# Two layers of linear attention and a Mish block on one core: key folds in two packets, two fetches and one product moved

## The chip, the cores and the metric

The kernel runs on one core of a Trainium2 chip. The metric is the device time of one execution in microseconds (us), as the median of several runs. The core has five engines that take their instructions in order: TensorE (PE, with its weight loads shown apart as PEld), VectorE (DVE), ScalarE (ACT), GpSimd (POOL) and SyncE (SP), which issues the DMA transfers here. [...]

## The reference, cut to what matters

The input x has 2048 rows of 640 numbers. The program runs two layers, each made of an attention part A and a dense part B, both with a residual:

```python
x = x + _A_ref(_layernorm(x), A_wqkv, A_w_phi, A_wo)
x = x + _B_ref(_layernorm(x), B_w1, B_b1, B_w2)
# and both once more
```

A makes q, k and v with 32 heads of 20, and turns q and k by one 20 x 20 matrix per head (`w_phi`). The features of a head are the softmax of the result beside the softmax of its negative. Then `kv = phi_k^T v`, `z = sum of phi_k`, and the output of a row is `phi_q kv / (phi_q z + 1e-6)`, multiplied by `wo`. B is `mish(x w1 + b1) w2` with 1536 hidden columns.

## The kernel before, in words

**Blocks and stages.** Rows are worked in NB = 8 blocks of 256 (BT = 2 tiles of 128). Each layer has three stages: `attend_first` (norm, keys, values, queries, and the sum `kva` over all rows), `attend_second` (the average of each row, `wo`, the residual, the statistics of the next norm) and `dense` (part B). Every number stands as a high and a low float32r part, so each product takes three matmuls (`project_half`, L385: high x high, high x low, low x high), five chunks of 128 deep.

**Folding.** Instead of turning q and k by `w_phi`, the kernel multiplies the weights by it once: `fold_part` (L257) is a float32 matmul of one group of six heads for one chunk k, and `fold_end` (L272) takes the result out of PSUM, as a copy on ACT (L275, the high part) and a subtraction on DVE (L276, the low part). A fold has five chunks k and two column halves c; one pair (k, c) takes three `fold_part`s. The query folds are in a block `written()`, in which the engines keep the order of the code. The key folds are `fold_phi` (L278), called in block 0 ahead of the first keys (L586).

**PSUM.** There are two `mm` tiles of two banks each and four `one` tiles of one bank. A product that finds no free tile waits until ACT and DVE have emptied one. `fold_phi` gives an even k an `mm` tile and an odd k two `one` tiles.

**Stage one, per block** (L565): six kinds in a fixed list, for block 0 of layer 0 `q0, v0, v1, k0, q1, k1`. For each kind the products are issued, and `advance()` (L447) takes every earlier generator one step further: `features` (L402) copies the products (L409), then takes maximum and minimum (L416) and the differences (L417, L419), then the exponential, then sums, reciprocal and quotient (L425, L426, L427); `queries` then transposes on DVE (L478) and writes the result to `e_d` in four transfers (L481). `fetch_normed` (L438) fetches the next block's rows and makes their statistics (L295, L297, L304, L305, L307); `normed` (L345) normalizes them, and `nxt.step()` (L316) transposes them on PE (L325), with a copy on ACT (L330) and a subtraction on DVE (L331).

**What sets the order.** Outside the written block a planner orders each engine's list, from the order of the code and a model of durations. `tc.issue_after(ins)` puts the instructions traced in it that run on the engine of `ins` behind `ins`; those on other engines stay free. In stage two PE and SP keep the order of the code (L728), and the planner orders the rest.

**Start of layer 0** (L499): SP fetches the rows, `w_phi` and the weights; the statistics of block 0 are made; PE folds q's first half for k = 0 to 3 (L524); then come the first `fold_end` (L527), the normalization of block 0 (L529 on ACT, L530 on DVE), two more `fold_end`s, the transposes and the first half of q0's product (L544). The second half folds follow with the splits of v's weights between them (`make_v`, L546), and then q0's second half (L556).

**Stage two** (L728): `rest()` finishes the last queries of stage one; `load(b)` (L639) reads block b of `e_d` into two `big` tiles and an `ol` tile; `average` (L676, products at L690) makes the rows' averages; `Transposed(...).all()` turns them; `Rows.half` (L717) multiplies by half of `wo`, adds the residual rows `xs[b]` (L720) and takes statistics (L721). The rows are fetched with `fetch` (L430) into one of two `xt` buffers, `xs[0]` at L733 and `xs[b + 1]` at L767. `tail()` (L671) takes `rest()` a step further. Blocks 0 and 1 are averaged before the loop; inside it the order on PE is: first half for tile 0, second half for tile 0, transposes of block b + 1, both halves for tile 1, then averages for b + 2 and b + 3 in every second block.

Of the kernel before, what the change touches and what calls it, by code (L numbers as in the profile page):

```python
# [25 lines left out]
BT = 2  # L26
# [18 lines left out]
def kernel(  # L45
# [71 lines left out]
    last_act, in_written, last_low, last_load, last_recip = [None], [False], [None], [None], [None]  # L117
# [139 lines left out]
    def fold_part(ps, k, t, bd, raw):  # L257

        r, rows = raw[t]
        heads = rows // DH  # L260
        n = DL * (6 * (t % 3) if t < 5 else 10)
        nc.tensor.matmul(ps[:, n:n + heads * DL].rearrange("p (j d) -> p j d", d=DL), r[:rows, k * P:(k + 1) * P],
                         bd[:rows, t, :rows].rearrange("p (j d) -> p j d", d=DH)[:, :, :DL], start=True, stop=True)

# [7 lines left out]
    def fold_end(ws, ps, k, c):  # L272
        n0, n1 = (0, 18 * DL) if c == 0 else (18 * DL, QK)
        hi, lo = ws[k][0][:, n0:n1], ws[k][1][:, n0:n1]
        nc.scalar.activation(hi, ps[:, :n1 - n0], AF.Copy)  # L275
        nc.vector.tensor_tensor(lo, ps[:, :n1 - n0], hi.bitcast(F32), op=ALU.subtract)  # L276

    def fold_phi(ws, bd, raw):  # L278

        pss = {}  # L280
        for k, c in ((0, 0), (1, 0), (2, 0), (3, 0), (0, 1), (1, 1), (2, 1), (3, 1), (4, 0), (4, 1)):
            if c == 0:
                mm = None if k % 2 else mm_tile()
                pss[k] = [one_tile(), one_tile()] if k % 2 else [mm[:, 0], mm[:, 1]]
            ps = pss[k][c]
            for t in range(3 * c, 3 * c + 3):
                fold_part(ps, k, t, bd, raw)
            fold_end(ws, ps, k, c)
# [96 lines left out]
    def project_half(ps, xts, t, ws, col, c, ks=range(KD), w=HC):  # L385
        sl = slice(t * P, (t + 1) * P)
        cs = slice(col + c * w, col + (c + 1) * w)
        for k in ks:
            h, l, wh, wl = xts.hs[k], xts.ls[k], ws[k][0][:, cs], ws[k][1][:, cs]
            for n, (a, r) in enumerate(((h, wh), (h, wl), (l, wh))):  # L390
                nc.tensor.matmul(ps[:, :w], a[:, sl], r, start=(k == 0 and n == 0),  # L391
                                 stop=(k == KD - 1 and n == 2))
# [42 lines left out]
    def attend_first(layer, x_src, first):  # L435


        def fetch_normed(b):  # L438
            if layer:
                return load_turned(n2_d[b], [row_tile] * 3, nc.gpsimd)  # L440
            xt = fetch(x_src, b) if b > 1 else early
            norm_scale(b, [norm_stats(t, xt) for t in range(BT)])
            return xt
# [55 lines left out]
        if first is None:  # L499
            with written():  # L500
# [23 lines left out]
                for t in range(3):  # L524
                    for k in range(KD - 1):
                        fold_part(pcs[k], k, t, bd, raw_q)
                fold_end(q_ws, pcs[0], 0, 0)  # L527
# [3 lines left out]
                                        op0=ALU.mult, op1=ALU.add)  # L531
                fold_end(q_ws, pcs[1], 1, 0)
# [32 lines left out]
        for b in range(NB):  # L565
# [15 lines left out]
            for n, (kind, t) in enumerate(order):  # L581
                t = int(t)
                i = b * BT + t
                if b == 0 and n == (1 if layer else 3):
                    if layer == 0:
                        fold_phi(kv_ws, bd, raw)  # L586
                    kva = one_tile()
                    nc.vector.memset(kva[:, :360], 0.0)
                if b == NB - 1 and n == 3:
                    loaded = {0: load(0)}  # L590
                if b + 1 < NB:
# [8 lines left out]
                if b == NB - 1 and n == 3:  # L600
# [36 lines left out]
        return kva, o_ws, loaded, rest()  # L637
# [28 lines left out]
    def attend_second(x_src, x_dst, acc, fetches, makes, fetch_next, begin_next):  # L666
        kva, o_ws, loaded, rest = acc
# [60 lines left out]
        with tc.manual_schedule(engines={mybir.EngineType.PE, mybir.EngineType.SP}):  # L728
# [4 lines left out]
            xs = {0: fetch(x_src, 0)}  # L733
# [22 lines left out]
            for b in range(NB):  # L756
# [9 lines left out]
                if b + 1 < NB:  # L766
# [8 lines left out]
                if b == NB - 2:  # L775
                    ahead = begin_next()
                if b + 1 < NB:
# [3 lines left out]
                r1.half(0, one_tile())  # L781
# [256 lines left out]
```

## Time and profile before

| | |
|---|---|
| runs | 1360.75 us median of 3 (1360.6 to 1360.98) |
| profiled execution | 1362.07 us |
| its span, first to last instruction | 1360.3 us |
| granted TensorE clock | 1.000 over the span |
| ACT busy, POOL busy | 575.6 us, 462.9 us |
| DMA | 174.11 MB, mean 128 GB/s |

Every kind of line is a view of one profiled execution. In a **timeline** a line is: start, us, engine, line of the kernel, operation, output <- input with their shapes, xcount, and in square brackets how long the engine had been idle just before, and what ended that. In the list of **waits** it is: who waited, for whom, total us, times, longest. A line of **windows** gives a stretch, the busy us of PE, PEld, DVE, ACT and POOL (with instruction counts), the granted clock, the busy share of the 16 DMA engines and GB/s. SPq is SP's issue of a transfer, not the transfer. Tile names: `mm` and `one` in PSUM, `r2h/r2l` the query weights, `r1h/r1l` the key and value weights, `xth/xtl` the transposed rows, `big` and `r` the features, `xn` normalized rows or averages.

### The profile page before, as it was taken

What the parts mean: (1) busy time and instruction counts of PE and PEld (TensorE: products, weight loads), DVE (VectorE), ACT (ScalarE), POOL (GpSimd) and SP (SyncE); (2) the same over time, 40 slices, a digit from 0 to 9 for tenths busy, and PEclk for the clock granted to TensorE, in tenths of its full rate; (3) what the DMA queues carried; (4) which work ended last, traced back from release to release, by engine and by line L of the source; (5) the groups of instructions that cost most, each with busy time, mean ns of one, the idle gap of its engine ahead of it and who ended that gap; (6) DMA issues with size and microseconds to landing.
All of it is one profiled execution on the core that took longest, in us unless ns stands there. A gap on an engine that the chain in (4) does not pass through costs nothing.

```text
span 1360.3 us, 30985 instructions
## 1 busy us (share of the span) xinstructions
PE 1347.8 (99%) x12896; PEld 1336.8 (98%) x12896; DVE 1061.9 (78%) x1799; ACT 575.6 (42%) x967; POOL 462.9 (34%) x417
## 2 busy tenths in 40 slices
PE   9999999999999999999999999999999999999999
PEld 8899999999999999999999999999999999999998
DVE  5888988886687887778769788878668776677775
ACT  4444344312454545445443334332235444454443
POOL 2355654434222222222225555644251211111112
PEclk9999999999999999999999999999999999999999
DMA  9543433797714442244563534559974321333200
GB/s 336 153 107 79 98 92 85 206 287 271 222 42 98 117 110 76 60 107 99 145 210 78 121 79 89 97 116 290 280 248 136 78 61 44 91 98 97 65 33 20
DMA packets 352629, 174.11 MB, mean 128 GB/s; under 512 B 287449, under 2 KB 324041, under 8 KB 352489
## 3 DMA queue, kind: packets, MB, share of 16 engines
q1 hardware_dynamic: 352489, 172.14, 46.8%
q8 instruction: 101, 1.65, 0.5%
q14 instruction: 39, 0.32, 0.1%
HBM read 106.23 MB, written 65.86 MB: 127 GB/s over the span
## 4 chain that ended last, share of the span: by engine, by line
PE 91%; DVE 4%; DMA 1%; POOL 1%; issue 0%; ACT 0%; SPq 0%; DVEq 0%; POOLq 0%
PE one L813 25%; PE mm L391 25%; PE mm L864 24%; PE one L391 11%; PE mm L690 2%; PE one L325 2%; PE one L464 1%; DVE r L425 1%; PE one L864 1%; DVE m L416 1%; DMA ol<-e_d 1%; PE one L690 1%; DVE r L419 1%; POOL big L427 0%; DMA big<-e_d 0%
## 5 line engine op out<-in xcount | busy, mean ns | idle before, releaser
L864 PE MATMUL mm<-r2h,ol 128*128 128x320 f32 x1240 | 296.1, 309 | 0.0
L839 POOL TENSOR_TENSOR ol<-big,ol 128x512 fp32r<-128x512 f32 (+1 forms) x98 | 130.9, 1336 | 477.9 <-ACT ol L838 419.8
L813 PE MATMUL one<-xtl,r1h 128*128 128x256 f32 x960 | 268.2, 279 | 0.0
L813 PE MATMUL one<-xth,r1l 128*128 128x256 f32 x960 | 268.0, 279 | 0.0
L813 PE MATMUL one<-xth,r1h 128*128 128x256 f32 x960 | 265.9, 279 | 0.0
L864 PEld LDWEIGHTS mm<-r2h,ol 128*128 128x128 f32 x1240 | 212.4, 188 | 0.0
L864 PE MATMUL mm<-r2l,ol 128*128 128x320 f32 x620 | 191.2, 309 | 0.0
L391 PE MATMUL mm<-r1h,xth 128*128 128x304 f32 (+1 forms) x600 | 185.2, 309 | 1.5 <-DVE r1l L276 1.5
L391 PE MATMUL mm<-r1l,xth 128*128 128x304 f32 (+1 forms) x600 | 183.8, 306 | 0.0
L391 PE MATMUL mm<-r1h,xtl 128*128 128x304 f32 (+1 forms) x600 | 183.5, 306 | 0.2 <-POOL xtl L331 0.2
L813 PEld LDWEIGHTS one<-xtl,r1h 128*128 128x128 f32 x960 | 180.4, 188 | 0.0
L813 PEld LDWEIGHTS one<-xth,r1l 128*128 128x128 f32 x960 | 180.4, 188 | 0.0
L813 PEld LDWEIGHTS one<-xth,r1h 128*128 128x128 f32 x960 | 179.6, 188 | 0.0
L828 DVE TENSOR_SCALAR big<-big 128x512 f32<-128x512 f32 (+1 forms) x98 | 56.9, 580 | 110.3 <-ACT big L826 110.1
L427 POOL TENSOR_TENSOR r<-r,r 128x1280 f32<-128x1280 f32 x32 | 77.2, 2412 | 127.0 <-DVE r L426 112.0
L830 ACT ACTIVATE big<-big,two 128x512 f32<-128x512 f32 (+1 forms) x98 | 70.1, 716 | 116.2 <-DVE big L829 116.2
L838 ACT ACTIVATE ol<-big 128x512 fp32r<-128x512 f32 (+1 forms) x98 | 60.9, 622 | 137.7 <-DVE big L837 137.6
L826 ACT ACTIVATE big<-one,b1s 128x256 f32<-128x256 f32 x192 | 80.8, 467 | 89.2 <-PE one L813 88.7
L864 PEld LDWEIGHTS mm<-r2l,ol 128*128 128x128 f32 x620 | 116.5, 188 | 0.0
L391 PEld LDWEIGHTS mm<-r1h,xth 128*128 128x128 f32 x600 | 112.8, 188 | 2.6 <-DVE r1l L276 1.7
L391 PEld LDWEIGHTS mm<-r1h,xtl 128*128 128x128 f32 x600 | 112.8, 188 | 0.4 <-POOL xtl L331 0.4
L391 PEld LDWEIGHTS mm<-r1l,xth 128*128 128x128 f32 x600 | 112.8, 188 | 0.1
(155 smaller groups left out, 3144.3 us busy)
## 6 DMA issues: line engine op xcount, KB each, us to landing
e_d<-r SPq DMA_DIRECT2D x128, 160.0 KB, 4.1
big<-e_d SPq DMA_DIRECT2D x32, 640.0 KB, 8.1
x_d<-xt SPq DMA_DIRECT2D x23, 640.0 KB, 4.2
xt<-x_d SPq DMA_DIRECT2D x22, 640.0 KB, 5.4
n_d<-xn SPq DMA_DIRECT2D x168, 80.0 KB, 2.4
xt<-in_x SPq DMA_DIRECT2D x16, 640.0 KB, 4.3
xn<-x_d SPq DMA_DIRECT2D x28, 320.0 KB, 4.3
v<-n_d SPq DMA_DIRECT2D x30, 256.0 KB, 3.1
```

Of the source, the lines that this page charges most:

```text
L325: nc.tensor.transpose(ps[:, c, t * P:(t + 1) * P], self.rows[t][:, (c0 + c) * P:(c0 + c + 1) * P], ident)
L391: nc.tensor.matmul(ps[:, :w], a[:, sl], r, start=(k == 0 and n == 0), stop=(k == KD - 1 and n == 2))
L416: nc.vector.tensor_reduce(m[:, s], eh[:, 1], axis=AX.X, op=op)
L427: nc.gpsimd.tensor_tensor(eg, eg, r.unsqueeze(2).to_broadcast([P, 2 * H, DH]), op=ALU.mult)
L690: nc.tensor.matmul(po[c][64 * q:64 * q + 64, GW * j:GW * j + w], phs[g][:n, s0:s0 + 64], kvb[:n, g, :w], start=True, stop=True)
L813: nc.tensor.matmul(ph[:, j, :], l, r, start=(n == 0), stop=(n == 3 * KD - 1))
L826: exps[0] = nc.scalar.activation(part(ta, 0)[:, j - js.start], ph[:, j, :], AF.Exp, bias=b1s[:, 2 * pr + j:2 * pr + j + 1]).ins
L828: nc.vector.tensor_scalar_min(e, e, E_CAP)
L830: nc.scalar.activation(r, n, AF.Ln, bias=two)
L838: nc.scalar.activation(ah[:, js], n, AF.Copy)
L839: nc.gpsimd.tensor_tensor(al[:, js], n, ah[:, js].bitcast(F32), op=ALU.subtract)
L864: ins = nc.tensor.matmul(pys[t][c][:, :HC], (ah, ah, al)[n][:, j, t * P:(t + 1) * P], w, start=(f == 0 and n == 0), stop=(f == KF - 1 and ...
```

## The change

It has four parts.

1. In the written start, the first `fold_end` of the query folds is put behind the two normalizations of block 0.
2. The key folds are called in two packets: (0,0), (1,0), (2,0), (3,0) between v0 and v1, and (4,0), (0,1), (1,1), (2,1), (3,1), (4,1) between v1 and k0. Two folds at a time share an `mm` tile (the last two take `one` tiles), and their `fold_end`s follow both. Every packet, and every kind's products in block 0, is put behind the last product before it on PE. From the fifth kind on, `advance()` in block 0 is put behind the last `fold_end` on DVE, and so are the statistics of block 3.
3. `xs[0]` and `xs[1]` are fetched in stage one's last block, right behind `load(0)`, in both layers; the two later fetches of these blocks go.
4. In stage two's block 0, in both layers, the first half for tile 1 is put ahead of the transposes of block 1.

The cut diff:

```diff
@@ fold_part
-        nc.tensor.matmul(ps[:, n:n + heads * DL]...
+        ins = nc.tensor.matmul(ps[:, n:n + heads * DL]...
+        last_product[0] = ins.ins
@@ fold_end
-        nc.vector.tensor_tensor(lo, ps[:, :n1 - n0], hi.bitcast(F32), op=ALU.subtract)
+        last_fold[0] = nc.vector.tensor_tensor(lo, ps[:, :n1 - n0], hi.bitcast(F32), op=ALU.subtract).ins
-    def fold_phi(ws, bd, raw):
-        pss = {}
-        for k, c in ((0, 0), (1, 0), (2, 0), (3, 0), (0, 1), (1, 1), (2, 1), (3, 1), (4, 0), (4, 1)):
...
+    def fold_phi(ws, bd, raw, parts):
+        for n in range(0, len(parts), 2):
+            mm = mm_tile() if n < 4 else None
+            pair = list(zip(parts[n:n + 2], [one_tile(), one_tile()] if mm is None else [mm[:, 0], mm[:, 1]]))
+            with tc.issue_after(last_product[0]):
+                for (k, c), ps in pair:
+                    for t in range(3 * c, 3 * c + 3):
+                        fold_part(ps, k, t, bd, raw)
+            for (k, c), ps in pair:
+                fold_end(ws, ps, k, c)
@@ project_half
-                nc.tensor.matmul(ps[:, :w], a[:, sl], r, ...)
+                last_product[0] = nc.tensor.matmul(ps[:, :w], a[:, sl], r, ...).ins
@@ fetch_normed
-            norm_scale(b, [norm_stats(t, xt) for t in range(BT)])
+            with (tc.issue_after(last_fold[0]) if b == 3 else nullcontext()):
+                norm_scale(b, [norm_stats(t, xt) for t in range(BT)])
@@ attend_first, written start
-                fold_end(q_ws, pcs[0], 0, 0)
                 xn = [row_tile() for _ in range(BT)]
...
+                fold_end(q_ws, pcs[0], 0, 0)
                 fold_end(q_ws, pcs[1], 1, 0)
@@ attend_first, loop over the kinds
+                if b == 0 and layer == 0 and n in (2, 3):
+                    fold_phi(kv_ws, bd, raw, ((0, 0), (1, 0), (2, 0), (3, 0)) if n == 2 else
+                             ((4, 0), (0, 1), (1, 1), (2, 1), (3, 1), (4, 1)))
                 if b == 0 and n == (1 if layer else 3):
-                    if layer == 0:
-                        fold_phi(kv_ws, bd, raw)
...
                     loaded = {0: load(0)}
+                    xs = {n: fetch(x_src, n) for n in range(2)}
...
-                if b == NB - 1 and n == 3:
+                if b == 0 and not layer:
+                    with tc.issue_after(last_product[0]):
+                        next(g)
+                    with (tc.issue_after(last_fold[0]) if n > 3 else nullcontext()):
+                        advance()
+                elif b == NB - 1 and n == 3:
@@ attend_second
             loaded[1] = load(1)
-            xs = {0: fetch(x_src, 0)}
...
-                if b + 1 < NB:
+                if 0 < b < NB - 1:
                     xs[b + 1] = fetch(x_src, b + 1)
...
+                if b == 0:
+                    r1.half(0, one_tile())
                 if b + 1 < NB:
                     nxt = Transposed(rows.pop(b + 1)).all()
                 if b == 2:
                     tail()
-                r1.half(0, one_tile())
+                if b > 0:
+                    r1.half(0, one_tile())
                 r1.half(1, one_tile())
```

More of the change, by code (lines that the diff above doesn't have):

```diff
@@ L390, in project_half @@
             for n, (a, r) in enumerate(((h, wh), (h, wl), (l, wh))):
-                nc.tensor.matmul(ps[:, :w], a[:, sl], r, start=(k == 0 and n == 0),
-                                 stop=(k == KD - 1 and n == 2))
+                last_product[0] = nc.tensor.matmul(ps[:, :w], a[:, sl], r, start=(k == 0 and n == 0),
+                                                   stop=(k == KD - 1 and n == 2)).ins
     def both(ps, w=HC):
@@ L635, in rest @@
                 advance()
-        return kva, o_ws, loaded, rest()
+        return kva, o_ws, loaded, xs, rest()
     def load(b):
```

14 lines of the change are left out of this document (4 added, 10 removed).

## The prediction

> **What bounds the kernel now.** I read the page first: its span and the busy line.
>
> ```profile
> span 1360.3 us, 30985 instructions
> PE 1347.8 (99%) x12896; PEld 1336.8 (98%) x12896; DVE 1061.9 (78%) x1799; ACT 575.6 (42%) x967; POOL 462.9 (34%) x417
> ```
>
> TensorE (PE) is idle for 1360.3 - 1347.8 = 12.5 us. The change takes no product away, so its gain can only come out of these 12.5 us. The second view is the list of PE's waits, for 0 to 60 us and then for the first stretch of stage two in layer 0 and in layer 1.
>
> ```profile
> PE mm L391 <- DVE r1l L276: 1.5, 1, 1.5
> PE mm L262 <- DVE r1l L276: 1.4, 1, 1.4
> PE one L325 <- ACT xn L131: 0.9, 1, 0.9
> PE one L391 <- DVE xt L720: 1.4, 2, 0.7
> PE mm L690 <- issue: 1.7, 2, 1.2
> ```
>
> Columns: who waited, for whom, us in total, times, longest. Each of the first four waits lies at a place that the diff touches; they are 0.9 + 1.4 + 1.5 + 1.4 = 5.2 us, the ceiling of what can be taken away directly. The fifth has no edit of its own. The third view, the busy time by stretch of 10 us (columns: PE, PE's weight loads, DVE, ACT, POOL, clock, DMA share, GB/s), says what PE lacks and when.
>
> ```profile
> 20.00:30.00 10.00, 10.00 (x71) 10.00 (x70) 8.47 (x22) 3.42 (x8) 2.86 (x6) 1.00 1.04 371
> 30.00:40.00 10.00, 7.13 (x62) 6.74 (x61) 7.36 (x19) 6.61 (x15) 3.69 (x4) 1.00 0.93 345
> 40.00:50.00 10.00, 10.00 (x74) 10.00 (x75) 6.65 (x14) 2.36 (x5) 1.30 (x5) 1.00 0.85 209
> 60.00:70.00 10.00, 10.00 (x131) 9.76 (x130) 9.99 (x12) 5.94 (x8) 5.79 (x4) 1.00 0.20 68
> ```
>
> The two waits on L276 are the 2.87 us missing at 30 to 40 us. From 40 us on PE has no gap until stage two, so what is won early should stay won; but DVE is full at 60 to 70 us, and that is where an earlier PE could meet a new limit (the slower rival).
>
> **Part 1: fold_end of the first query fold behind the two normalizations.** The timeline of 6 to 19 us:
>
> ```profile
> 6.90 3.05 PE L262 MATMUL mm<-big,raw 120*128 120x114 f32 x24 [0.68 <-DMA raw<-in_wqk_t]
> 8.18 0.23 DVE L307 SCALAR_TENSOR_TENSOR stats<-mv,stats 128x1 f32<-128x1 f32 x2 [1.10 <-POOL stats L305]
> 9.54 0.46 ACT L275 ACTIVATE r2h<-mm 128x342 fp32r<-128x342 f32 x1 [7.54 <-PE mm L262]
> 9.89 0.91 ACT L131 ACTIVATE xn<-xt,stats 128x640 f32<-128x640 f32 x1
> 10.70 0.79 ACT L275 ACTIVATE r2h<-mm 128x342 fp32r<-128x342 f32 x2
> 10.85 1.25 PE L325 MATMUL one<-ident,xn 128*128 128x128 f32 x8 [0.91 <-ACT xn L131]
> 11.70 0.60 ACT L131 ACTIVATE xth<-one 128x512 fp32r<-128x512 f32 x1 [0.21 <-PE one L325]
> ```
>
> The statistics are ready at 8.41, but ACT takes its list in order and sits waiting for the fold until 9.54; the normalization comes after. With the two swapped, ACT normalizes from 8.45 to 9.36 and copies the fold at 9.54 as now. DVE normalizes the other half at the same time, also without the fold ahead of it. PE's folds end at 6.90 + 3.05 = 9.95 and the transposes follow at once: the 0.9 us go. What is late next is ACT's copy of the transposes: it started 0.85 us after them, at 11.70, so 10.80 now, and ACT has done the two other fold copies (0.79 us from about 9.9) by 10.7. **Term: -0.9 us**, bounds 0 and -0.91.
>
> **Part 2: the key folds in two packets, PE's order fixed.** In before, PE's holes while it waited for the query weights were filled with parts of the key fold and with v0.
>
> ```profile
> 17.87 0.68 PE L262 MATMUL mm<-big,raw 120*128 120x114 f32 x4
> 18.38 0.58 PE L262 MATMUL one<-big,raw 120*128 120x114 f32 x4
> 18.98 0.39 PE L391 MATMUL mm<-r2h,xth 128*128 128x304 f32 x1
> 20.67 0.43 DVE L276 TENSOR_TENSOR r2l<-one,r2h 128x266 fp32r<-128x266 f32 x1
> 24.32 0.30 PE L391 MATMUL mm<-r2h,xtl 128*128 128x304 f32 x1
> ```
>
> Fixed order means q0's second half, then v0, four folds, v1, six folds, k0. Price of the lost filling: PE's last query fold no longer has the key fold of 17.87 ahead of it (0.51 us), and all is 0.91 us early, so q0's products start at 18.98 - 0.91 - 0.51 = 17.56. Fifteen take 2.1 us (71 products fill the 10 us from 20 to 30: 0.141 each), to 19.7. But the last ones need DVE's r2l, ready at 21.10 - 0.91 = 20.2; two products of 0.14 follow: 20.5. **New idle: 20.5 - 19.7 = 0.8 us.** Queued behind on PE is v0; its weight splits are DVE's next work, and v0 needs its fourth and fifth only 1.3 and 1.8 us after it starts, when they stand. In exchange q0 ends at 20.5 instead of 24.46, and DVE gets q0's reductions 4 us earlier.
>
> What goes, from the timeline of 31 to 40 us:
>
> ```profile
> 33.31 1.49 DVE L425 TENSOR_REDUCE r<-r 128x64 f32<-128x1280 f32 x1 [1.49 <-ACT r L134]
> 35.70 0.67 PE L262 MATMUL mm<-big,raw 120*128 120x114 f32 x4 [1.39 <-DVE r1l L276]
> 37.84 1.61 DVE L295 BATCH_NORM_STATS2 bn<-xt 128x6 f32<-128x320 f32 x4
> 39.36 0.42 DVE L276 TENSOR_TENSOR r1l<-mm,r1h 128x266 fp32r<-128x266 f32 x1
> 39.83 0.41 PE L391 MATMUL mm<-r1h,xth 128*128 128x304 f32 x1 [1.49 <-DVE r1l L276]
> ```
>
> Seven folds in a row filled the two mm tiles and the one tiles; DVE first waited for q0's exponentials, did L425, and only then emptied them: PE lost 1.39. Then block 3's statistics (1.61) stood ahead of a subtraction that frees a tile: 1.49. Afterwards at most four folds stand together, v1's 30 products (4.2 us) lie between the packets, about twice the four subtractions of the first packet (L276 took 0.42 for 266 columns, so an estimated 0.54 for 342: 2.2 us); L425 is ready about 4 us earlier; block 3's statistics come after the last subtraction. The second packet takes 6 x 0.67 = 4.0 us of PE; its first pair, whose tile k0 needs, is out 2.7 us before k0. ACT's two copies and DVE's two subtractions (about 0.5 each) fit. So both waits are costed at nothing, hidden by v1 and by the four later folds; without that cover they return at the same 1.4 to 1.5 each. What is late next: k0's second half needs the last subtraction, 2.1 us after k0 starts, against about 1 us. advance() held behind the last fold puts k0's reductions and q0's transpose behind it on DVE; they wait for k0's products anyway. Fold and transpose counts are equal. **Term: -(1.39 + 1.49) + 0.8 = -2.1 us**, bounds +0.8 (both waits return) and -2.9 (the new idle is filled).
>
> **Part 3: stage two's first block, in both layers.**
>
> ```profile
> 263.42 1.48 DVE L425 TENSOR_REDUCE r<-r 128x64 f32<-128x1280 f32 x1
> 264.53 1.26 PE L325 MATMUL one<-ident,xn 128*128 128x128 f32 x10
> 264.81 0.48 DVE L720 TENSOR_TENSOR xt<-one,xt 128x320 f32<-128x320 f32 x1
> 265.94 0.48 DVE L720 TENSOR_TENSOR xt<-one,xt 128x320 f32<-128x320 f32 x1
> 266.48 0.41 PE L391 MATMUL one<-r2h,xth 128*128 128x320 f32 x1 [0.69 <-DVE xt L720]
> 276.35 0.42 PE L391 MATMUL one<-r2h,xth 128*128 128x320 f32 x1
> 928.78 0.41 PE L391 MATMUL one<-r2h,xth 128*128 128x320 f32 x1 [0.69 <-DVE xt L720]
> ```
>
> Two halves and three transposes take five one tiles, and there are four: r1's first half waits for L720. With that half ahead of the transposes it takes the fourth tile at 264.53 and runs 2.2 us, and L720's end at 266.42 lies before the second transpose group needs the tile. Block 1 reads the transposes at 276.35; they end at about 268.0 instead of 265.8, with some 8 us to spare. **Term: -0.69 x 2 = -1.4 us**, bounds -1.4 and 0 (the wait moves to r1's second half, if DVE takes L478, 1.46 us, ahead of the third L720).
>
> The fetches pass on SP: one goes ahead of eight e_d writes and load(1), the other also ahead of load(2), load(3) and the weight rows.
>
> ```profile
> 228.67 0.99 SPq L646 DMA_DIRECT2D big<-e_d  x2
> 235.00:240.00 5.00, 5.00 (x36) 5.00 (x35) 5.00 (x6) 2.54 (x4) 0.96 (x1) 1.00 0.01 4
> 256.00:262.00 6.00, 5.95 (x109) 5.54 (x104) 5.28 (x17) 1.58 (x4) 0.00 (x0) 1.00 1.06 360
> ```
>
> They leave the stretch behind load(1), where DMA is full (1.06 from 256 to 262), for one behind load(0) at 228.67, beside a stretch at 0.01. Both xt buffers are free then: block 7's rows were normalized in block 6. 1.3 MB at 360 GB/s are 3.6 us, which the quiet hides. I cost this at nothing; without the quiet, load(0), issued just ahead, would land up to 3.6 us later, and its first reader is stage two. Loads 2 and 3 land earlier; nothing showed a wait of PE on them.
>
> One place is open, in layer 1, where averages stall inside a group of four alike:
>
> ```profile
> 919.49 0.25 PE L690 MATMUL mm<-kvb,ol 80*64 80x42 f32 x1 [1.21 <-issue]
> 918.00:924.00 6.00, 4.79 (x77) 4.41 (x72) 4.08 (x12) 1.36 (x3) 0.00 (x0) 1.00 1.03 347
> ```
>
> No semaphore falls between the third and the fourth, so I suspect code arriving late behind a full DMA (1.03). I take 0, because loads 2 and 3 fill the stretch without the rows too; bounds -1.7 (both stalls go) and +1.2 (one more such stall in layer 0, which has none yet). [...]
>
> **Sum.** -0.9 - 2.1 - 1.4 = -4.4 us. The profiled execution took 1362.07 us for its span of 1360.3 (1.77 around it, which no edit touches); its span would be 1355.9. The runs' median is 1360.75, so **1356.4 us** (0.32% faster).
>
> **The rivals.** About 0.2%, 2.7 us, is what a measurement of this kernel can tell from no change.
>
> - *The waits return in block 0.* The planner puts DVE's queue in another order, and k0 or a fold waits for a tile again for 2.9 us in all. For: the two waits came from just such an order, and nothing fixes L425 against the folds. Against: DVE has 1.53 + 2.64 + 3.35 = 7.5 us free from 20 to 50 us. Then -0.9 + 0.8 - 1.4 = -1.5: **1359.2**.
> - *Stage two gives nothing*: the tile wait moves to r1's second half, or the planner issues the fetches no earlier and L720 stays behind L425. Then -3.0: **1357.8**.
> - *The code stalls go as well* with the rows out of the way: -1.7 more, **1354.7**. [...]
> - *Slower: DVE becomes the bound in blocks 1 and 2.* The pins hold block 3's statistics (1.61) and everything of advance() from the fifth kind on (k0's reductions, q0's transpose) behind the last fold. DVE's 7.5 free us before 50 us then pass unused, that much work slides into the full stretch from 60 us, and there each us shows on PE: 7.5 - 4.4 = +3.1, **1363.9**. It turns slower once over 4.4 of the 7.5 us are lost so. For: 9.99 of 10 us are taken at 60 to 70. Against: PE is full there too and waits for nothing, and the last fold comes about 3 us earlier than before, not later.
>
> **How the numbers follow.** Forecast 0.58, waits return 0.17, stage two nothing 0.10, code stalls go 0.06, slower 0.09. The range 1354.4 to 1360.2 holds all but the last; its low end is the sum with the code stalls and a little of the new idle filled, its high end the first rival with one us of further loss (a stall of 1.2 us in layer 0 among it). Under 1358.0 lie nearly all of the forecast, over half of the second rival and the third: faster 0.66. Slower by over 0.2% is the last rival and a little of the first's loss: 0.10. Within: 0.24.
>
> **What would show it.** In the list of PE's waits: L325 on xn gone (part 1); L262 and L391 on r1l gone, and a new wait of about 0.8 of L391 on r2l L276 near 20 us (part 2); L391 on L720 gone in both layers (part 3); in the timeline of SP two xt fetches near 230 and 890 us; PE's stretch of 30 to 40 us at 10.0. I am wrong if PE's waits on r1l stand at another time, if stage one shows gaps after 50 us, or if the issue waits of L690 change by a us.

## The result and the profile after

The changed kernel takes **1358.65 us** (median of 19 runs, 1357.4 to 1360.06), the kernel before 1361.29 us (median of 19 runs, 1360.53 to 1364.36). The ratio is 0.998, with a 95% interval of 0.9972 to 0.9987: 2.6 us faster. The profiled execution of the changed kernel took 1358.37 us, 3.70 us less than that of before (1362.07 us). So the two profiles show about a microsecond more than the medians do; the last part of the comparison says where it comes from.

The page of the changed kernel, its span and busy line:

```profile
span 1356.6 us, 30976 instructions
PE 1348.5 (99%) x12896; PEld 1337.0 (99%) x12896; DVE 1058.8 (78%) x1799; ACT 576.0 (42%) x967; POOL 464.0 (34%) x417
```

PE's idle time is now 1356.6 - 1348.5 = 8.1 us instead of 12.5. The list of PE's waits of the changed kernel:

```profile
PE mm L700 <- issue: 1.5, 2, 1.0
PE mm L393 <- DVE r2l L278: 0.4, 1, 0.4
PE one L327 <- DVE r1l L278: 0.2, 1, 0.2
PE mm L393 <- ACT xth L132: 0.2, 1, 0.2
PE mm L393 <- DVE xtl L333: 0.2, 1, 0.2
```

All four waits that the prediction aimed at have left the list (0.9, 1.4, 1.5 and 2 x 0.7 us). In their place stand small ones. Two of them are the story of part 1: L393 on `xth` and `xtl` is q0's first half waiting for ACT and DVE at 12.20 and 12.93, 1.4 and 2.1 us after the place (10.85) of the wait that was removed. The two on `r2l` and `r1l` belong to part 2. The issue waits of the averages (now L700) are nearly as they were.

Where did the 3.7 us come from? The same product is looked up in both traces, and the difference of its start is taken. Timeline of PE, before:

```profile
15.23 0.56 PE L262 MATMUL one<-big,raw 120*128 120x114 f32 x4
44.80 0.30 PE L391 MATMUL mm<-r2h,xth 128*128 128x304 f32 x1
252.37 1.39 PE L690 MATMUL mm<-kvb,big 120*64 120x63 f32 x40
296.33 1.39 PE L690 MATMUL mm<-kvb,big 120*64 120x63 f32 x40
912.70 0.44 PE L690 MATMUL mm<-kvb,big 120*64 120x63 f32 x6
958.63 1.39 PE L690 MATMUL mm<-kvb,big 120*64 120x63 f32 x40
```

and after:

```profile
15.17 0.56 PE L263 MATMUL one<-big,raw 120*128 120x114 f32 x4
42.74 0.30 PE L393 MATMUL mm<-r2h,xth 128*128 128x304 f32 x1
250.29 1.39 PE L700 MATMUL mm<-kvb,big 120*64 120x63 f32 x40
293.43 1.39 PE L700 MATMUL mm<-kvb,big 120*64 120x63 f32 x40
909.86 0.44 PE L700 MATMUL mm<-kvb,big 120*64 120x63 f32 x6
955.15 1.39 PE L700 MATMUL mm<-kvb,big 120*64 120x63 f32 x40
```

The rows are: the first fold behind q0's first half; q1's first product; in each layer the first average of stage two, and the averages for blocks 4 and 5, behind the place of parts 3 and 4. Differences from row to row give each stretch its share:

| stretch | forecast | shown by the two profiles |
|---|---|---|
| to the end of q0's first half (part 1) | -0.9 | -0.06 |
| to q1's first product (part 2) | -2.1 | -2.00 |
| rest of stage one, layer 0 | 0 | -0.02 |
| stage two, layer 0 (parts 3 and 4) | -0.7 | -0.82 |
| to stage two of layer 1 | 0 | +0.06 |
| stage two, layer 1 (parts 3 and 4) | -0.7 | -0.64 |
| to the end | 0 | -0.2 |
| sum | -4.4 | -3.7 |

One line is wrong: part 1 gave 0.06 us in place of 0.9. The window of 30 to 40 us, where PE had 7.13 us of products, is all but full now:

```profile
30.00:40.00 10.00, 9.77 (x78) 9.46 (x77) 7.75 (x23) 7.03 (x15) 3.67 (x6) 1.00 0.77 267
```

What took part 1's gain shows on ACT. Timeline of ACT, changed kernel:

```profile
8.52 0.92 ACT L132 ACTIVATE xn<-xt,stats 128x640 f32<-128x640 f32 x1 [6.52 <-DVE stats L309]
9.81 0.46 ACT L277 ACTIVATE r2h<-mm 128x342 fp32r<-128x342 f32 x1 [0.38 <-PE mm L263]
10.85 0.80 ACT L277 ACTIVATE r2h<-mm 128x342 fp32r<-128x342 f32 x2 [0.58 <-DVE r2l L278]
11.54 0.60 ACT L132 ACTIVATE xth<-one 128x512 fp32r<-128x512 f32 x1
```

The normalization did come first, as meant, and done at 9.44. But the second fold copy, which the prediction let start at 9.9, starts at 10.85: ACT sits idle for 0.58 us, released by DVE's `r2l`. This copy reads the second half of the `mm` tile whose first half DVE is just subtracting, and the program has a semaphore wait there, ACT's second copy behind DVE's first subtraction. It had it in the kernel before too. There the 0.91 us of normalization stood in that wait and cost ACT almost nothing: from the start of the first copy to that of the second it was 10.70 - 9.54 = 1.16 us with the normalization between them, and it is 10.85 - 9.81 = 1.04 us without. Taken out, it uncovered the wait.

### The profile page after: what moved, and what is told of

The parts are those of the page before. It is cut to its first block, busy times and chain, and to the rows that moved or that the text cites. A ratio compares the mean times of both kernels' runs of the same rounds, so it can differ in the third digit from the quotient of the medians.

```text
span 1356.6 us, 30976 instructions
## 1 busy us (share of the span) xinstructions
PE 1348.5 (99%) x12896; PEld 1337.0 (99%) x12896; DVE 1058.8 (78%) x1799; ACT 576.0 (42%) x967; POOL 464.0 (34%) x417
## 4 chain that ended last, share of the span: by engine, by line
PE 91%; DVE 6%; DMA 1%; POOL 1%; issue 0%; ACT 0%; SPq 0%; DVEq 0%; POOLq 0%
PE mm L393 26%; PE one L825 25%; PE mm L876 24%; PE one L393 11%; PE mm L700 2%; PE one L327 2%; PE one L467 2%; DVE r L427 1%; DMA raw<-in_wqk_t 1%; DVE xn L713 1%; PE one L876 1%; DVE m L418 1%; DVE r L421 1%; DMA r<-in_wqk_t 0%; DVE xtl L333 0%; PE one L700 0%
## 5 line engine op out<-in xcount | busy, mean ns | idle before, releaser
L393 PE MATMUL mm<-r1h,xth 128*128 128x304 f32 (+1 forms) x600 | 185.1, 309 | 0.0
L393 PE MATMUL mm<-r1l,xth 128*128 128x304 f32 (+1 forms) x600 | 183.8, 306 | 0.0
L393 PE MATMUL mm<-r1h,xtl 128*128 128x304 f32 (+1 forms) x600 | 183.5, 306 | 0.2 <-POOL xtl L333 0.2
L393 PEld LDWEIGHTS mm<-r1h,xth 128*128 128x128 f32 x600 | 112.8, 188 | 0.9
L393 PEld LDWEIGHTS mm<-r1h,xtl 128*128 128x128 f32 x600 | 112.8, 188 | 0.4 <-POOL xtl L333 0.4
L393 PEld LDWEIGHTS mm<-r1l,xth 128*128 128x128 f32 x600 | 112.8, 188 | 0.1
```

Source lines behind the costliest of these rows:

```text
L393: last_product[0] = nc.tensor.matmul(ps[:, :w], a[:, sl], r, start=(k == 0 and n == 0), stop=(k == KD - 1 and n == 2)).ins
```

## The experiments

**Theory and rivals.** The theory: part 1 fails because ACT and DVE empty the two halves of one tile in turn; part 2 pays by the order of DVE's subtractions; of parts 3 and 4 only the moved half pays. Rivals: part 1 does work and something later gives it back; the fetches matter; the issue waits are data or DMA traffic, not code. Times of one part alone lie within 1.3 us of the kernel before, and their intervals reach about 1.2 us to each side: none of the four is a change that the times alone show. The traces tell them apart.

### Each part alone

**only_norm**: the kernel before with part 1 alone.

```diff
-                fold_end(q_ws, pcs[0], 0, 0)
                 xn = [row_tile() for _ in range(BT)]
...
+                fold_end(q_ws, pcs[0], 0, 0)
                 fold_end(q_ws, pcs[1], 1, 0)
```

> Part 1 alone on the kernel before (first fold_end behind the two normalizations). Theory M: the two halves of one mm tile are emptied one after the other (ACT's copy of the second half waits until DVE has subtracted the first), the normalization stood in that wait for nothing, and the swap only uncovers it. Then ACT idles 0.5 to 0.6 us ahead of the second copy, q's first fifteen products end at 15.1 to 15.3 us as before (15.23), and the time is -0.2 to 0 us. Rival F (the prediction's step): the swap gives 0.9 us and it is the fixed order of part 2 that lost it. Then these products end near 14.3 us and the time is -0.9 us.

Measured: 1361.54 us against 1361.73, ratio 0.9999 (0.999 to 1.0008), span 1360.6. Timeline of ACT:

```profile
8.54 0.92 ACT L131 ACTIVATE xn<-xt,stats 128x640 f32<-128x640 f32 x1 [6.54 <-DVE stats L307]
11.37 0.80 ACT L275 ACTIVATE r2h<-mm 128x342 fp32r<-128x342 f32 x2 [0.58 <-DVE r2l L276]
```

PE's wait on `xn` is gone, the same 0.58 us of ACT's waiting stands behind it, and q0's first half ended at 15.69 (the weights landed late in this run, at 8.70). So the gain is lost inside q0's first half, not somewhere later.

**only_packets**: the kernel before with part 2 alone.

```diff
-    def fold_phi(ws, bd, raw):
+    def fold_phi(ws, bd, raw, parts):
...
+                if b == 0 and layer == 0 and n in (2, 3):
+                    fold_phi(kv_ws, bd, raw, ((0, 0), (1, 0), (2, 0), (3, 0)) if n == 2 else
```

> Part 2 alone on the kernel before (key folds in two packets, order fixed). Theory M: all of what stage one's block 0 gained is here: the waits of 1.39 and 1.49 us on r1l go, one of about 0.4 on r2l comes near 21 us, q1's first product starts near 42.8 us (before 44.80), time -2.0 us. Rival F: block 0 gains 1.2 us (2.1 less the 0.9 of part 1 that it gives back), q1's first product near 43.6 us.

Measured: 1360.73 us, ratio 0.9994 (0.9985 to 1.0002), span 1357.5. The waits on `r1l` of 1.39 and 1.49 us are gone, the wait on `xn` (0.9) and both on `xt` (0.7 each) stay, and q1 starts at 42.96 instead of 44.80: 1.84 us. Part 2 earns its share without part 1 in this trace. The median moved by 1.0 us, half of the 2.0 that were expected. Its profiled execution was the fastest of its runs (1359.25 us) and that of before was slower than the median; what differs from run to run is told below, with own_tiles_norm.

**only_fetch**: the kernel before with part 3 alone (`xs[0]` and `xs[1]` fetched behind `load(0)`).

> Part 3 alone (both residual blocks fetched in stage one's last block). Theory M: the waits on L720 stay at 0.69 in both layers, because DVE's list puts L720 behind L425 whenever the rows come; perhaps 0.3 us less at the averages of block 1 in layer 0. Time 0 to -0.3 us. Rival: the late rows made L720 late; then both waits go and the time is -1.4 to -1.9 us.

Measured: 1361.0 us, ratio 0.9994 (0.9985 to 1.0002), span 1359.2. The list of waits still has L391 on `xt` with 1.4 us in two waits. The shorter span comes from block 0, which this edit does not touch: there the wait at 35 us was 0.20 instead of 1.39 (below).

**only_half**: the kernel before with part 4 alone.

```diff
+                if b == 0:
+                    r1.half(0, one_tile())
                 if b + 1 < NB:
                     nxt = Transposed(rows.pop(b + 1)).all()
...
-                r1.half(0, one_tile())
+                if b > 0:
+                    r1.half(0, one_tile())
```

> Part 4 alone (tile 1's first half ahead of the transposes in block 0 of stage two). Theory M: both waits on L720 go, 0.94 us of PE's time each with the end of the last transpose, and 0.3 us each come back at the first half of tile 1 in block 1: time -1.3 us. Rival (the fetch is needed for it): waits stay or move to tile 1's second half, time 0.

Measured: 1360.44 us, ratio 0.9993 (0.9984 to 1.0002), span 1359.4. Both waits on `xt` are gone; 0.32 us comes back in block 1 of each layer, as in the changed kernel. The moved half carries all of stage two's gain, the fetches none of it that a trace shows.

**half_two**: the changed kernel, with part 4 for block 1 too.

```diff
-                if b == 0:
+                if b < 2:
                     r1.half(0, one_tile())
...
-                if b > 0:
+                if b > 1:
```

> The changed kernel with part 4 for blocks 0 and 1. Theory M: the wait of 0.32 us behind the transposes of block 1 goes in both layers, and moves to block 2 with at most the same size, because it is the same fight for four one tiles: time -0.6 to 0 us. Rival: it comes from DVE's list in block 1 and comes back at tile 1's second half: 0.

Measured: 1358.63 us, ratio 0.9979 (0.9969 to 0.9988), span 1355.9. The waits of 0.32 us are gone in both layers. A shorter one comes in their place: block 1 has no averages behind its transposes, so block 2's first product now follows them closely and its weight load waits for their low part. In layer 0:

```profile
283.33 0.19 PEld L393 LDWEIGHTS one<-r2h,xth 128*128 128x128 f32 x1 [0.21 <-DVE xtl L333]
```

In layer 1 the same load waits 0.21 us at 944.35. The span is 0.7 us shorter, but about 0.6 of it arises at the first averages of layer 1, where the stalls called issue were shorter in this execution and which the edit does not touch. The median does not move by a measurable amount.

### Part 1 with the chain taken away

A wait can't be struck out alone, so the tiles were changed: the first four query folds get four separate tiles, and the fifth the spare half of the first. No copy then follows a subtraction of the same tile.

```diff
-                pcs = [mm[0][:, 0], mm[0][:, 1], mm[1][:, 0], mm[1][:, 1], one_tile()]
+                pcs = [mm[0][:, 0], mm[1][:, 0], one_tile(), one_tile(), mm[0][:, 1]]
```

**own_tiles**: the changed kernel with this edit.

> The changed kernel, but the first four query folds stand in four PSUM tiles (two mm, two one), and the fifth in the spare half of an mm tile, so no copy waits for the subtraction of a neighbour. Theory M: ACT's second copy follows the first without the idle of 0.58 us, the transposes' copies come 0.5 to 0.7 us earlier, q's first fifteen products end 0.5 to 0.8 us earlier than in the changed kernel (15.17, as counted from the landing of the raw weights), q1's first product starts 0.3 to 0.8 us earlier than 42.74. Time -0.3 to -0.8 us against the changed kernel. Rival F (something else, the late landing of the raw weights for one, holds these products): nothing moves.

Measured: 1357.76 us (1357.01 to 1359.67), ratio 0.9972 (0.996 to 0.9984), span 1356.3. q0's first half ends at 14.30 instead of 15.17, and q1 starts at 41.88 instead of 42.74: the 0.9 us that the prediction gave to part 1 are there once the tiles are apart, and in the changed order they still stand at q1. Not all of it lasts. The first average of stage two is 0.67 us early (249.62 against 250.29); in the third average PE waits 0.29 us for `load(1)` (254.02), which the changed kernel did not, and at the end 0.3 us of the span are left. The intervals of the two ratios overlap, so the trace shows the gain at q1, and the times do not show one at the end.

**own_tiles_before**: the kernel before with this edit; **own_tiles_norm**: the kernel before with this edit and part 1.

> The kernel before, with one edit: the first four query folds take four separate tiles and the fifth the spare half of the first; the order of norm and folds is that of before. Theory M (in before the normalization stands in ACT's wait for DVE's subtraction of the other half of the same tile): without that wait the normalization still comes behind the first fold copy, so PE's wait on xn stays (0.8 to 1.1 us near 10.8), and q0's first half ends within 0.2 us of before's 15.2 (later if the weights land late). Rival (the tiles alone bring the gain of own_tiles): q0's first half ends near 14.3.

> The kernel before with the same four tiles and with part 1 (the first fold copy behind the normalizations), nothing else of the change. Theory M: both edits together bring what the prediction gave part 1 alone: no wait of PE on xn at 10.8, no gaps of 0.46, 0.35 and 0.16 us among q0's products, and q0's first half ends 0.8 to 0.95 us earlier than in own_tiles_before (near 14.3, as far as the weights land alike). Rival (something of part 2 to 4 is needed): it ends near 15.2, as part 1 alone did.

Measured: 1360.28 us (one run, span 1358.5) and 1363.05 us (one run, span 1361.2). Timeline of own_tiles_before, ACT and PE:

```profile
10.07 0.91 ACT L131 ACTIVATE xn<-xt,stats 128x640 f32<-128x640 f32 x1
11.03 1.25 PE L325 MATMUL one<-ident,xn 128*128 128x128 f32 x8 [0.68 <-ACT xn L131]
```

and of own_tiles_norm:

```profile
8.36 0.92 ACT L131 ACTIVATE xn<-xt,stats 128x640 f32<-128x640 f32 x1 [6.36 <-DVE stats L307]
9.19 0.79 ACT L275 ACTIVATE r2h<-mm 128x342 fp32r<-128x342 f32 x2
9.86 0.46 ACT L275 ACTIVATE r2h<-one 128x342 fp32r<-128x342 f32 x1
24.17 1.67 DVE L295 BATCH_NORM_STATS2 bn<-xt 128x6 f32<-128x320 f32 x4 [2.60 <-DMA xt<-in_x]
35.35 0.67 PE L262 MATMUL mm<-big,raw 120*128 120x114 f32 x4 [2.11 <-DVE r1l L276]
```

In the second, ACT's copies follow one another without a pause. Because the weights land at another time in each run, the fair measure is from the end of the first folds on PE to the end of q0's first half:

| | shared tile | separate tiles |
|---|---|---|
| fold copy first | 15.23 - 9.95 = 5.28 us (before) | 15.40 - 10.35 = 5.05 us (own_tiles_before) |
| normalization first | 15.17 - 10.23 = 4.94 us (changed kernel) | 13.81 - 9.80 = 4.01 us (own_tiles_norm) |

Either edit alone is worth 0.2 to 0.35 us, both together 1.27; with the tiles apart the order alone brings 5.05 - 4.01 = 1.04 us, with a shared tile 0.34. (The 0.34 us of the changed kernel do not show in its 15.17, since its folds ended 0.28 us later.) Other traces with the same tiles and order repeat these sizes: 4.95 in only_norm (15.69 - 10.74), 4.01 in own_tiles (14.30 - 10.29). That settles part 1: the order was right and the shared tiles kept it from paying.

The last two rows of own_tiles_norm show something else. It was 1.4 us ahead of before at q0's first half (13.81 against 15.23) and 0.35 us ahead at the fold of 35 us, which is as much as its rows landed earlier. In the order of before, DVE stands in front of block 1's statistics until its rows land, and everything behind follows at fixed distances. Timeline of DVE, before:

```profile
24.52 1.67 DVE L295 BATCH_NORM_STATS2 bn<-xt 128x6 f32<-128x320 f32 x4 [1.53 <-DMA xt<-in_x]
```

From this row to PE's next fold at 35.70 it is 11.18 us. In own_tiles_norm it is 35.35 - 24.17 = 11.18 us, in only_fetch (rows at 23.70, fold at 34.88) 11.18, in only_norm (24.68, 35.85) 11.17. So with this order a gain from ahead of 24 us is given back at 35 us, as far as a wait stands there: part 1 could have paid little without part 2. And the wait that part 2 removed is as long as the landing and PE's own arrival make it: 1.39 us in the profile of before, but 0.60 in only_norm, 0.79 in only_half and 0.20 in only_fetch, none of which edits this place.

The changed order hangs on something else. In the order of before, q1's first product follows the start of block 1's statistics by 20.28 us: 44.80 - 24.52, in only_fetch 43.98 - 23.70, in only_norm 44.96 - 24.68. In the changed order it follows the end of q0's first half by 27.6 us wherever the rows land: 42.74 - 15.17 in the changed kernel, 42.96 - 15.38 in only_packets (statistics at 23.30), 42.88 - 15.27 in half_two (24.66), 41.88 - 14.30 in own_tiles (24.34). So part 2 took q1 off the landing, and what that is worth depends on the landing. An estimate from these rows: with the changed order's 27.6 us behind their own first half, q1 would have come 2.0 us earlier in before, 1.6 in only_half, 1.7 in only_norm and 0.8 in only_fetch, 1.5 on average.

### Part 2 without PE's fixed order

**no_pins**: the changed kernel without the two orders on PE.

```diff
-            with tc.issue_after(last_product[0]):
+            with nullcontext():
                 for (k, c), ps in pair:
...
-                    with tc.issue_after(last_product[0]):
-                        next(g)
+                    next(g)
```

> The changed kernel without the two orders that put each packet of key folds and each kind's products of block 0 behind the last product on PE; the packets, their shared tiles and the orders on DVE stay. Theory P (the gain of part 2 needs PE's fixed order): the planner mixes folds and products again, PE waits 1 to 2 us more for emptied tiles between 20 and 45 us than the changed kernel's 0.94 us, and its first product of q1 comes 1 to 2 us later than 42.74. Rival T (shared tiles and the DVE order alone do it): q1 starts within 0.4 us of 42.74 and the waits stay under 1.2 us.

Measured: 1362.08 us (one run), span 1360.2, q1's first product at 46.43. Timeline and windows:

```profile
39.36 0.62 PE L393 MATMUL mm<-r1h,xth 128*128 128x304 f32 x1 [2.36 <-DVE r1l L278]
```

```profile
40.00:50.00 10.00, 10.00 (x55) 10.00 (x55) 4.32 (x8) 1.25 (x3) 0.93 (x3) 0.72 0.95 264
```

The wait on `r1l` is back, 2.36 us long, and q1 comes 3.7 us later, twice what was expected. The second row says why: behind the wait the granted clock was 0.72 over these 10 us, and PE did 55 products where before did 74 at 1.00. In the one execution seen, part 2's gain is gone without PE's fixed order.

### The issue waits of layer 1

**code_shift**: the changed kernel with 22 instead of 30 warming transposes ahead of everything, so that each instruction of PE lies 8 products earlier in the program.

> The changed kernel with 22 warm-up transposes in place of 30, so that every later matmul of PE stands 8 matmuls (16 instructions with their weight loads) earlier in the program. Theory C (the stalls called issue in layer 1 are code that arrives late at a block border): the first stall moves from the 7th matmul of the first average to the 15th, the second from the last matmul of the third average to the 8th of the ten transposes behind it; they stay 128 matmuls apart. Rival D (a semaphore or a transfer of data): both stay at the same matmul. Time unchanged in both.

Measured: 1357.79 us (one run), span 1356.0. The first average and the end of the third, changed kernel:

```profile
909.86 0.44 PE L700 MATMUL mm<-kvb,big 120*64 120x63 f32 x6
910.75 1.21 PE L700 MATMUL mm<-kvb,big 120*64 120x63 f32 x34 [0.46 <-issue]
916.63 0.25 PE L700 MATMUL mm<-kvb,ol 80*64 80x42 f32 x1 [1.01 <-issue]
```

and code_shift:

```profile
910.17 0.68 PE L700 MATMUL mm<-kvb,big 120*64 120x63 f32 x14
911.16 0.97 PE L700 MATMUL mm<-kvb,big 120*64 120x63 f32 x26 [0.31 <-issue]
917.00 0.55 PE L327 MATMUL one<-ident,xn 128*128 128x128 f32 x3 [0.18 <-issue]
```

The first stall moves from behind the 6th product of the group to behind the 14th, the second from the last `ol` product of the average into the transposes behind it: both 8 products on in the work. Counted from the start of the program they stay: behind 9033 and 9161 matmuls, in before, in the changed kernel and here. A stall that stays with the place in the program and not with the data points to code arriving late; that is the author's inference, since the traces show the place alone. The two places are 128 matmuls apart, but that distance makes no rule: counting on by 128 matmuls, the places next to these two (906.45 and 929.67 us) show no gap in the changed kernel, and neither do those in layer 0's stage two; these two, with 0.46 and 1.01 us idle, are the exceptions. They are not in every trace: in only_half, own_tiles_norm and own_tiles_half_two PE runs through both places, and instead waits 1.22 to 2.80 us for `big` between them. From the first average the next 174 products take 9.15 us in only_half, which has the wait of 1.84 us and no stall, and 9.31 in before, which has both stalls and no such wait. So a stall that goes can leave a wait for `load(1)` of the same size.

**loads_late**: the changed kernel with `load(2)`, the first weight fetch and `load(3)` put behind the last average ahead of the loop.

```diff
-            loaded[2] = load(2)
-            fetches[0]()
...
+            loaded[2] = load(2)
+            fetches[0]()
```

> The changed kernel with load(2), the first weight rows of the dense part and load(3) issued behind the fourth average instead of among the averages. Theory C: with DMA empty while PE runs through the averages, code arrives in time, and the two stalls of 0.67 and 1.23 us in layer 1 shrink to under 0.3 each; time -1.0 to -1.6 us at the start of block 0's products in layer 1, unless the averages of block 2 then wait for load(2). Rival: the stalls are code that arrives late whatever DMA carries (PE runs through short matmuls faster than code can come): they stay at 0.6 and 1.2 us.

Measured: 1358.9 us (one run), span 1357.1. Start to start, the two places take 0.68 and 1.08 us, against 0.68 and 1.23 in the changed kernel. But the DMA share from 911 to 917 us only fell from 0.93 to 0.82, so it does not tell whether the stalls come from a full DMA. That stays open.

### Both additions

**own_tiles_half_two**: the changed kernel with separate tiles and with the moved half in blocks 0 and 1.

> The changed kernel with the two additions that helped in the traces: four separate tiles for the first query folds (q0's first half 0.87 us earlier) and the half for tile 1 ahead of the transposes in block 1 too (two waits of 0.31 us gone). If both carry to the end: span 1356.6 - 0.9 - 0.6 = 1355.1, and 1.0 to 1.5 us less than the changed kernel's median, ratio to the kernel before near 0.997. Rival (the end is set by waits that vary by run, the early gain is given back to landings): no more than 0.5 us less than the changed kernel.

Measured: 1357.29 us (1356.58 to 1359.43, 6 runs), ratio 0.997 (0.9958 to 0.9982), the best median of the study, 1.4 us under the changed kernel. The intervals of the two ratios overlap, so that it beats the changed kernel is likely and not shown. Its profiled execution was the longest of its six (1359.43 us, span 1357.6), and the timeline says why:

```profile
915.60 1.11 PE L700 MATMUL mm<-kvb,big 120*64 120x63 f32 x20 [2.80 <-DMA big<-e_d]
916.82 2.40 PE L327 MATMUL one<-ident,xn 128*128 128x128 f32 x10
```

PE arrived at stage two of layer 1 at 908.68, 1.2 us earlier than the changed kernel, and waited 2.80 us for `load(1)`. Its transposes then took 2.40 us where the changed kernel's take 1.31, at a granted clock of 0.53 (from 915.8 to 919.4 us). So both the expectation (the gain holds up to layer 1) and its rival (landings take it back) came true in this execution.

## Why the prediction was right or wrong

**What bounds the kernel: right.** The gain came out of PE's idle time, at the places named. That "what is won early should stay won" held for the 2.06 us of the changed kernel at q1, which are 2.08 at stage two; of the 0.9 us that own_tiles won besides, 0.6 were given back later, most of it to a wait for `load(1)`.

**Part 1, -0.9 us: wrong.** The step that failed is "ACT has done the two other fold copies (0.79 us from about 9.9) by 10.7". They ran from 10.85 to 11.65. The prediction took the duration of the copies from a row and their start from the list before them, and did not ask what they wait for besides ACT. That 0.79 us stood behind the normalization without a gap in the profile of before was no proof: the wait was covered by what was moved. Tiles of their own and the new order together bring 1.27 us.

**Part 2, -2.1 us: right in size by luck, partly wrong in its reason.** The two profiles show -2.0. The luck is the landing: in the profile that the prediction read, block 1's rows came late enough for a wait of 1.39 us, and by the estimate above other executions offer 0.8 to 1.7 us. The new idle of 0.8 us came as a wait of 0.39 us on `r2l` near 21 us, and 0.23 more at 37.83. But "L425 is ready about 4 us earlier" failed. Timeline of DVE, changed kernel:

```profile
24.22 1.67 DVE L297 BATCH_NORM_STATS2 bn<-xt 128x6 f32<-128x320 f32 x4 [1.72 <-DMA xt<-in_x]
30.01 0.51 DVE L278 TENSOR_TENSOR r1l<-mm,r1h 128x342 fp32r<-128x342 f32 x1
34.78 1.49 DVE L427 TENSOR_REDUCE r<-r 128x64 f32<-128x1280 f32 x1 [1.12 <-ACT r L135]
```

The reduction (L427 now) starts at 34.78, where it was 33.31: q0 ends early on PE, but DVE still stands in front of block 1's rows until 24.22. What helps is that the first subtractions of the key folds (30.01 and the next ones) now stand ahead of it, so no fold waits for it. "Block 3's statistics come after the last subtraction" did not come true either:

```profile
38.03 0.43 DVE L278 TENSOR_TENSOR r1l<-one,r1h 128x266 fp32r<-128x266 f32 x1
38.37 1.27 DVE L297 BATCH_NORM_STATS2 bn<-xt 128x6 f32<-128x320 f32 x3
39.56 0.42 DVE L278 TENSOR_TENSOR r1l<-mm,r1h 128x266 fp32r<-128x266 f32 x1
```

They come behind the one that is last in the code (38.03), but the planner put an earlier one behind most of them (39.56). It ends at 39.98, and k0, whose first half runs on PE from 38.24 without it, loses nothing.

**Parts 3 and 4, -1.4 us: right in size, because two errors nearly cancel.** The waits on `xt` are gone. Each had cost 0.94 us from product to product and not the 0.69 us of the list, and 0.3 us each comes back at the same line a block later; the weight load waits there for a tile:

```profile
278.94 0.19 PEld L393 LDWEIGHTS one<-r2h,xth 128*128 128x128 f32 x1 [0.31 <-DVE xt L730]
```

That leaves 0.62 us in each layer. The other 0.2 us of layer 0's 0.82 is a wait of before for `load(1)` near 256.5, which is absent in only_half too and so owes nothing to the fetches. The wait that comes back the prediction did not see: it looked at when block 1 reads the transposes, not at the tiles that block 1 itself needs. It also priced parts 3 and 4 as one; only_fetch and only_half show that the moved half alone does it. And the fetches do not lie where the prediction put them:

```profile
178.53 0.33 SPq L434 DMA_DIRECT2D xt<-in_x  x1
206.81 0.34 SPq L434 DMA_DIRECT2D xt<-in_x  x1
```

The planner issues them 20 and 48 us ahead of the last transfer of `load(0)` (226.62), so the collision that was weighed could not arise.

**The issue waits, 0: right.** In code_shift the stalls stay behind 9033 and 9161 matmuls while the work moves on by 8 products, which fits the suspicion that they are code. That late code causes them, or that it has borders as the expectation of code_shift takes it to, no run shows.

**The rivals.** No wait returned in block 0 with the change as made; no_pins shows that the first rival was near. Stage two gave 1.46 us, not nothing. The stalls called issue did not go (1.5 us of 1.7 are still in the list); by only_half, a part at least of their 1.7 us would have gone to a wait for `load(1)`. The slower case did not come: from q1 to stage two the two traces differ by 0.02 us, so DVE did not become the bound.

**The number.** 1356.4 was forecast, 1358.65 came, 2.25 us more. The 19 runs put the kernel before at 1361.29, 0.54 above the median that was known. In the profiles the change gave 3.7 of the 4.4 us: part 1 is 0.84 short, and the other stretches together are 0.14 over. The remaining 1.06 us is the choice of profile: that of before lay 0.78 us above its median (1362.07 against 1361.29) and that of after 0.28 below (1358.37 against 1358.65). A wait that varies from 0.2 to 1.39 us was taken at 1.39. By the estimate above that accounts for about 0.5 us (2.0 against 1.5 on average); where the rest comes from is not shown.

## What to carry to other kernels

When an instruction is moved out of a queue, look up what the next ones wait for besides their engine: the piece that is moved may have filled a wait that the profile then could not show (0.58 us here). A wait that hangs on a DMA's landing, as the one at 35 us here does (0.20 to 2.11 us in five traces), is worth its mean over runs, not its length in one profile, and here it took back a gain made ahead of it. Look in several traces at what the next stage follows at a fixed distance: that is what it hangs on. When a tile shortage is cured in one block, count the tiles of the next block too.

## What the runs showed of the hardware

**The granted clock fell to half in or behind some short idle stretches.** In no_pins it fell to 0.50 at 38.7 us, 1.7 us into an idle stretch of 2.36 us, and was back at 1.00 at 45.5. In own_tiles_norm, window by window:

```profile
34.40:35.20 0.80, 0.00 (x0) 0.00 (x0) 0.80 (x3) 0.42 (x2) 0.00 (x0) 1.00 0.33 133
35.20:36.00 0.80, 0.65 (x6) 0.65 (x7) 0.80 (x4) 0.00 (x0) 0.00 (x0) 1.00 1.01 381
36.00:36.80 0.80, 0.80 (x8) 0.80 (x7) 0.80 (x4) 0.39 (x1) 0.00 (x0) 0.69 1.02 383
36.80:37.60 0.80, 0.80 (x6) 0.80 (x6) 0.73 (x4) 0.60 (x1) 0.59 (x1) 0.50 0.98 365
40.00:40.80 0.80, 0.80 (x8) 0.80 (x7) 0.80 (x4) 0.00 (x0) 0.10 (x1) 1.00 1.00 371
```

PE was idle for 2.11 us up to 35.35, ran on at 1.00 for about a microsecond, then at 0.50 for 3.4 us. The same happened behind 2.80 us (own_tiles_half_two, 3.4 us at 0.50), and in layer 1 of own_tiles_norm behind waits of 1.22 and 0.29 us that ended 1.1 us apart; it did not behind this one of only_half:

```profile
918.76 0.80 PE L690 MATMUL mm<-kvb,big 120*64 120x63 f32 x20 [1.84 <-DMA big<-e_d]
```

So one wait is not like another: those of 1.39 and 1.49 us of the kernel before and the 1.84 us of only_half left the clock at 1.00, while 1.22 and 0.29 us of own_tiles_norm were followed by a drop; and in no_pins 2.36 us of waiting moved q1 by 3.7 us. The slow stretches lasted 3.4 us (three of them) or 6.8 (no_pins). What decides whether the clock falls, and when, these traces do not show.

**Two stalls called issue keep their places in the program.** They stand behind 9033 and 9161 matmuls in before, in the changed kernel and in code_shift. Places counted from these two in steps of 128 matmuls lie in the averages of layer 0 as well (252.27 and 269.76 us in the changed kernel), at a DMA share of 0.89 from 252 to 254 us, and show no gap there. Ten of the 14 traces list waits called issue on PE's averages or transposes, 0.2 to 1.7 us in sum; only_half, own_tiles_before, own_tiles_norm and own_tiles_half_two list none. The first stall of layer 1 falls into a microsecond with a DMA share of 0.51 (910 to 911 us), the second into one of 1.09. So neither short products nor a full DMA alone goes with a stall; what causes them stays open.
